# Attention into two MoE layers on one core: later weight decoding, P·V in two pieces per chunk, and the next head pair turned over three units

## The chip, the core and the metric

One core of a Trainium2 chip runs the whole kernel in one launch. The metric is device time in microseconds: the median of three runs before the change is 562.89 us (562.86 to 563.21). Besides these there is one profiled execution, whose instructions, waits and transfers are recorded with their times; it took 561.78 us, of which 559.7 us lie between its first and its last instruction.

## What is computed

```python
def _attn_ref(q, k, v):                       # 2 batches, 8 heads, 576 rows, 64 columns
    ...
    q_rot, k_rot = rotate(q), rotate(k)       # rotary positions
    scores = scale * np.matmul(q_rot, k_rot.transpose(0, 1, 3, 2))
    scores = scores - np.max(scores, axis=-1, keepdims=True)
    attn = np.exp(scores)
    attn = attn / (np.sum(attn, axis=-1, keepdims=True) + 1e-09)
    return np.matmul(attn, v)

def _moe_ref(x, w_in, w_out):                 # 1152 tokens, 512 -> 2048 -> 512
    h = x @ w_in
    g = np.maximum(h, 0.0) + np.log1p(np.exp(-np.abs(h)))
    return g @ w_out
# then _moe2_ref: skip test, gate, 8 experts of 512 -> 1024 -> 512, one expert for each token
```

The weights `w_in` and `w_out` arrive as 64-bit floats, which the kernel takes apart with integer operations ("decoding").

## The kernel before

**Stages.** Attention takes about the first 187 us of the profiled execution, then comes the first MoE layer (class `Moe1`), then the second (class `Moe2`). The change touches attention and the decoding of the first weights.

**Pairs and units.** The 16 heads of both batches are worked on as 8 pairs of heads: pairs 0 to 3 in batch 0, pairs 4 to 7 in batch 1. A pair has five units: four of 128 query rows for both heads (numbers 0 to 3), and one, "m", of the last 64 rows of both heads. There are 40 units, counted 0 to 39. In batch 0 their order is 0, 1, 2, 3, m; in batch 1 it is 2, 3, m, 0, 1. I say first, second, ... unit of a pair for the place in that order.

**One unit.** For each of the two heads a: S, matmuls that write scores into PSUM tile `s` (`s_mm`, L188; two such tiles exist); M, the row maximum on VectorE (`s_max`, L220); E, exp on ScalarE (`s_exp`, L228). One unit later the exponentials P are turned by TensorE in three groups T0 to T2 (`t_steps`, L286, into PSUM tiles `t`, of which there are three) and copied to `pt` by VectorE or ScalarE (H0 to H2, helper L74). The order of these steps inside a loop pass is written out in `ORDER` (L26). TensorE's order in the loop is as written; the other engines' order is set by a list scheduler, and each engine runs its list strictly in order.

**P·V.** Units are gathered in two chunks per pair. When a chunk's P is turned, its product with v is made in five jobs (`pv_mm`, L337; tiles `pv`, `vr`, `vd`), two jobs in each loop pass (the two J in `ORDER`). After the first job row sums are inverted (`norm`, tile `R`), after the fourth they are turned (`norm_out`, tiles `t..n`, `rb`), after the last the result x goes to `xh` and `xl` (`x_out`).

**Turning the next pair.** While a pair is worked on, the next one is prepared (`prepare`, L437): GpSimd rotates q and k (`rope_pair`; tiles `rt`, `rot`), TensorE turns q and k (`tq`, two times four transposes into `tq` tiles) and the last 64 rows (one transpose into a `tr` tile); ScalarE and VectorE split each into a high and a low half (`halves`, L139; tiles `qT`, `kT`, `qm`); then `stacks` (L173) issues eight copies on SyncE's queue from one place of on-chip memory to another, four for tile `qs` (128 KB each) and four for tile `ks` (288 KB each). The S matmuls of the next pair read `qs` and `ks`: the first head's S reads the two copies for a = 0, the second head's S the two for a = 1. `PREP` (L27) says in which unit of the pair each step is written: q and k rotations in the first, all turning and the copies in the second, loads in the fourth.

**First weights.** `Moe1.weights` (L470) loads 128 columns of `w_in` and 128 rows of `w_out` (tile `raw`, two buffers), decodes each on VectorE by L488, L489, L490 into `wt`, and splits it by a cast on ScalarE (L492) and a subtraction on VectorE (L493) into `w`. I call one load of the two a half. `W_AT` (L32) puts the first two weights behind loop passes 27 and 34, but nothing holds the scheduler to it; it places them where it expects their data.

Of the kernel before, what the change touches and what calls it, by code (L numbers as in the profile page):

```python
# [25 lines left out]
ORDER = "S0 R T0 M0 J H0 E0 S1 T1 H1 M1 J T2 H2 E1 Q".split()  # L26
PREP = ("qk", "t", "", "l", "")  # L27
# [3 lines left out]
W_AT = (27, 34)  # L31
# [12 lines left out]
class Attention:  # L44
# [45 lines left out]
    def load_pair(self, b, hp):  # L90
# [8 lines left out]
        self.pr[b, hp] = dict(xn=xn)  # L99
# [51 lines left out]
    def tq(self, b, hp):  # L151
        nc, p = self.nc, self.pr[b, hp]
        ident = self.cst["ident"]
        rot = p["rot"].rearrange("p i j h d -> p i j (h d)")
# [18 lines left out]
    def stacks(self, b, hp):  # L173

        p = self.pr[b, hp]
        qT, kT = p["qT"], p["kT"]
        p["qs"] = qs = self.wq.tile([128, 2, 512], F32R, name=f"qs{b}{hp}", tag="qs", bufs=2)
        p["ks"] = ks = self.wq.tile([128, 2, 2, 576], F32R, name=f"ks{b}{hp}", tag="ks", bufs=2)
        for a in range(2):
            r = slice(64 * a, 64 * a + 64)  # L180
            kc = slice(64 - 64 * a, 640 - 64 * a)
            for o in range(2):
                d = slice(64 * o, 64 * o + 64)
                self.nc.sync.dma_start(qs[d, a, :].bitcast(F32), qT[r, 0 if o == a else 1, :].bitcast(F32))
# [35 lines left out]
    def s_max(self, b, hp, u, a):  # L220
# [7 lines left out]
    def s_exp(self, b, hp, u, a):  # L228
# [12 lines left out]
        if u == "m":  # L241
            nc.gpsimd.tensor_scalar(P[:, 576:640], P[:, 512:576], 1.0, 1.0, op0=ALU.mult, op1=ALU.mult)
# [94 lines left out]
    def pv_mm(self, b, hp, c, z):  # L337
# [4 lines left out]
        if z == 2:  # L342
            nc.tensor.matmul(ps[:, 0:n], lhsT=p["vd"], rhs=pt[:, 4, 0:n], start=False, stop=False, skip_group_check=True)
            return
        i = (0, 1, None, 2, 3)[z]
        with self.tc.manual_schedule(engines={nc.tensor.engine}):
            for a in range(2):
                nc.tensor.matmul(  # L348
                    ps[64 * a : 64 * a + 64, 0:n], lhsT=p["vr"][:, a, i, :], rhs=pt[:, 5 * a + i, 0:n],
                    start=z == 0, stop=z == 4, skip_group_check=True,  # L350
                )
# [24 lines left out]
    def run(self, side=None):  # L376
# [12 lines left out]
        self.tq(0, 0)  # L389
        self.stacks(0, 0)  # L390
# [6 lines left out]
        for i in range(n + 7):  # L397
# [3 lines left out]
            ready, jobs = jobs[:2], jobs[2:]  # L401
# [3 lines left out]
            with order:  # L405
                for step in ORDER:
# [30 lines left out]
    def prepare(self, i, pairs):  # L437
# [3 lines left out]
        if pi + 1 == len(pairs):  # L441
            return
        nxt = pairs[pi + 1]
        for step in PREP[z]:
            if step == "q":
                self.rope_pair(*nxt, 0, g3)
# [730 lines left out]
```

## Time and profile before

| | |
|---|---|
| median of three runs | 562.89 us |
| the profiled execution | 561.78 us |
| its span, first to last instruction | 559.7 us |
| TensorE busy (matmuls) | 508.4 us, 91% |
| VectorE busy | 416.8 us, 74% |
| ScalarE busy | 326.5 us, 58% |
| GpSimd busy | 125.5 us, 22% |
| first S of pair 0, 1, 2, 3 at | 14.84, 34.58, 59.73, 87.68 us |
| first S of pair 4, 5, 6, 7 at | 107.73, 128.45, 148.27, 168.09 us |
| first matmul of the first MoE layer at | 187.02 us |

Shares over the whole span mix stages with different limits. For this change the stretch from 14.84 to 187.02 us counts, and in it the steps from one pair's first S to the next's. The granted clock of TensorE in a stretch is given as a share of 2.4 GHz; 0.50 is the lower of its two levels, 1.2 GHz.

### The profile page before, as it was taken

The numbers are of one execution on the slowest core, as the hardware profiler recorded it, in microseconds if no ns is written. First come the engines' busy times: TensorE is split into PE (matmuls) and PEld (weight loads), VectorE is DVE, ScalarE is ACT, GpSimd is POOL, SyncE is SP. The second block draws the span as 40 slices with busy tenths as digits, with TensorE's granted clock in tenths as the row PEclk, the third lists the DMA queues.
The fourth block names the chain that finished last, engine by engine and source line by source line (L and its number), as shares of the span: only waits on it lengthen the run. The fifth ranks groups of instructions, "written<-read, shape, count | busy, mean of one in ns | idle before, by whom it ended". The sixth has DMA issues, their size and how long they took to land. (4 is left out here: it accounts for less than half of the span.)

```text
span 559.7 us, 8595 instructions
## 1 busy us (share of the span) xinstructions
PE 508.4 (91%) x2858; PEld 394.7 (71%) x2858; DVE 416.8 (74%) x788; ACT 326.5 (58%) x711; POOL 125.5 (22%) x169
## 2 busy tenths in 40 slices
PE   6796969999999978877999999999999899999993
PEld 2664646667667646567889988989897577777772
DVE  7569886766666389998979994474785579887873
ACT  2565545567656265666566674575564378776860
POOL 5766393763411220000000000000020401220111
PEclk9898979999999999999999999999998999999998
DMA  7897473742550024434213430032205615695301
GB/s 184 196 238 191 133 188 104 182 98 66 125 122 2 2 84 150 117 124 138 75 46 116 142 112 0 1 112 77 80 22 193 245 55 187 224 334 180 97 19 36
DMA packets 42500, 67.17 MB, mean 120 GB/s; under 512 B 9312, under 2 KB 23904, under 8 KB 42448
## 3 DMA queue, kind: packets, MB, share of 16 engines
q1 hardware_dynamic: 38672, 59.59, 36.9%
q0 software_dynamic: 1440, 4.20, 2.0%
q10 hardware_dynamic: 2336, 2.74, 1.5%
q8 instruction: 26, 0.43, 0.3%
q14 instruction: 26, 0.21, 0.1%
HBM read 67.30 MB, written 7.15 MB: 133 GB/s over the span
## 5 line engine op out<-in xcount | busy, mean ns | idle before, releaser
L506 PE MATMUL h<-xh,w 128*128 128x320 f32 (+2 forms) x448 | 106.0, 317 | 6.6 <-DVE w L493 2.9
L543 PE MATMUL acc<-w,gh 128*128 128x512 f32 x288 | 76.9, 397 | 9.3 <-ACT gh L533 9.1
L506 PEld LDWEIGHTS h<-xh,w 128*128 128x128 f32 x448 | 75.5, 188 | 13.9 <-DVE w L493 4.8
L764 DVE TENSOR_TENSOR ws<-raw,ws 128x1024 fp32r<-128x1024 f32 x59 | 70.3, 1220 | 16.8 <-ACT ws L762 16.6
L224 DVE TENSOR_REDUCE m<-s 128x1 f32<-128x576 f32 x64 | 47.7, 755 | 27.6 <-PE s L215 23.9
L506 PE MATMUL h<-xl,w 128*128 128x320 f32 (+2 forms) x224 | 68.1, 313 | 0.0
L543 PEld LDWEIGHTS acc<-w,gh 128*128 128x128 f32 x288 | 52.1, 188 | 22.2 <-ACT gh L533 12.4
L237 ACT ACTIVATE P<-s,m 128x576 f32<-128x576 f32 x64 | 47.6, 744 | 29.9 <-DVE m L224 28.3
L302 PE MATMUL t<-ct,P 128*128 128x128 f32 x288 | 49.8, 287 | 15.1 <-DVE qT L146 6.0
L852 PE MATMUL y<-ws,hT 128*128 128x512 f32 x216 | 59.8, 415 | 0.9 <-DVE hT L838 0.2
L762 ACT CAST ws<-raw 128x1024 fp32r<-128x1024 f32 x59 | 59.2, 1060 | 2.3 <-DMA raw<-in_moe_w_dram 2.0
L302 PEld LDWEIGHTS t<-ct,P 128*128 128x128 f32 x288 | 35.1, 145 | 28.4 <-issue 10.6
L852 PEld LDWEIGHTS y<-ws,hT 128*128 128x128 f32 x216 | 39.2, 188 | 13.4 <-DVE ws L764 2.3
L606 POOL TENSOR_SCALAR sc<-lg 128x2 f32<-128x2 f32 (+1 forms) x3 | 0.9, 294 | 212.2 <-DVE lg L589 212.2
L215 PE MATMUL s<-ks,qs 128*128 128x288 f32 x240 | 47.3, 328 | 0.1
L348 PE MATMUL pv<-pt,vr 128*64 128x256 f32 (+1 forms) x256 | 46.0, 443 | 0.8 <-DVE x L358 0.5
L519 ACT ACTIVATE y<-h 128x320 f32<-128x320 f32 (+2 forms) x56 | 25.0, 447 | 36.5 <-PE h L506 32.1
L215 PEld LDWEIGHTS s<-ks,qs 128*128 128x128 f32 x240 | 35.6, 199 | 13.2 <-issue 5.2
L77 ACT COPY pt<-t 128x384 f32<-128x384 f32 x60 | 28.5, 475 | 25.8 <-PE t L302 21.6
L543 PE MATMUL acc<-w,gl 128*128 128x512 f32 x144 | 42.8, 395 | 0.5 <-DVE gl L534 0.4
L506 PEld LDWEIGHTS h<-xl,w 128*128 128x128 f32 x224 | 41.7, 188 | 2.0
L533 ACT CAST gh<-r 128x320 fp32r<-128x320 f32 (+2 forms) x56 | 24.6, 467 | 29.1 <-DVE r L531 29.1
(257 smaller groups left out, 934.8 us busy)
## 6 DMA issues: line engine op xcount, KB each, us to landing
raw<-in_moe_w_dram SPq DMA_DIRECT2D x68, 512.0 KB
ks<-kT SPq DMA_DIRECT2D x32, 288.0 KB
raw<-in_moe_w_in_dram SPq DMA_DIRECT2D x16, 512.0 KB
raw<-in_moe_w_out_dram SPq DMA_DIRECT2D x16, 512.0 KB
qs<-qT SPq DMA_DIRECT2D x32, 128.0 KB
wr<-in_moe_w_dram SPq DMA_DIRECT2D x5, 512.0 KB
x2d<-x SPq DMA_DIRECT2D x9, 256.0 KB
xn<-in_q_dram SPq DMA_DIRECT2D x8, 256.0 KB
```

Source lines behind the costliest of these rows:

```text
L77: self.nc.scalar.copy(out, in_)
L215: nc.tensor.matmul(ps[:, c, 0:288], lhsT=qs[:, a, uc], rhs=ks[:, a, x, 288 * c : 288 * c + 288], start=x == 0, stop=x == 1,)
L224: nc.vector.tensor_reduce(st["m"][:, a : a + 1], st["ps"][a][:, :, 0:288], axis=AX.XY, op=ALU.max, negate=True)
L237: nc.scalar.activation(P[:, 576 * a : 576 * a + 576].rearrange("p (c n) -> p c n", c=2), ps[:, :, 0:288], AF.Exp, bias=m[:, a : a + 1], ac ...
L302: nc.tensor.transpose(ps[:, 128 * i : 128 * i + 128], src, ident)
L348: nc.tensor.matmul(ps[64 * a : 64 * a + 64, 0:n], lhsT=p["vr"][:, a, i, :], rhs=pt[:, 5 * a + i, 0:n], start=z == 0, stop=z == 4, skip_gro ...
L506: nc.tensor.matmul(ps[c][:, 0:m], lhsT=w[:, 0, x, 128 * k : 128 * k + 128], rhs=src[:, k, c0 + m * c : c0 + m * c + m], start=z == 0, stop ...
L519: nc.scalar.activation(y[:, cs[c]], ps[c][:, 0:m], AF.Abs)
L543: nc.tensor.matmul(acc[t], lhsT=g[x][:, 128 * j : 128 * j + 128], rhs=w[:, 1, y, :], start=f == f0 and z == 0, stop=f == f1 and z == 2,)
L762: hi = nc.scalar.copy(w[:, 0], raw)
L764: self.did[T, c] = hi.ins, nc.vector.tensor_sub(w[:, 1], raw, w[:, 0].bitcast(F32)).ins
L852: nc.tensor.matmul(py, lhsT=ht[:, x, o : o + 128], rhs=w[:, y, 512 * j : 512 * j + 512], start=c == 0 and j == 0 and z == 0, stop=c == 3 a ...
```

## The change

1. Decoding of the first two weights is written in four halves behind loop passes 29, 31, 33 and 35, and on VectorE and ScalarE each half is tied to stand behind the last maximum of its pass (`tc.issue_after`).
2. P·V of a chunk is made in two jobs instead of five, one job in each loop pass instead of two: the first is the `vd` product and half of the `vr` products, the second the other half with `norm_out` and `x_out`. The loop has four closing passes instead of seven.
3. The next pair's q, k and last rows are turned in three units. From the third pair of the loop on (pairs 2 to 6 are the current ones): q in the first unit, k in the second, the last rows and the copies of `ks` in the third. While pair 1 is current: second, third, fourth unit. While pair 0 is current: q in the third, k and last rows in the fourth. The copies of `qs` are issued behind q's turn, those of `ks` behind the turn of the last rows.
4. Rotations on GpSimd and loads are made one pair earlier.
5. The copy of 64 columns of P in unit m moves from GpSimd to ScalarE.

```diff
-ORDER = "S0 R T0 M0 J H0 E0 S1 T1 H1 M1 J T2 H2 E1 Q".split()
-PREP = ("qk", "t", "", "l", "")
+ORDER = "S0 R T0 M0 H0 E0 S1 T1 H1 M1 J T2 H2 E1 Q".split()
+PREP = (("xR", "", "q", "krxv", "R"), ("", "q", "k", "rxvR", ""), ("q", "k", "r", "xvR", ""))
...
-W_AT = (27, 34)
+W_AT = (29, 31, 33, 35)
...
+    def tq(self, b, hp, i):
...
+        if i == 0:
+            p["qT"] = t = self.wq.tile([128, 2, 512], F32R, name=f"qT{b}{hp}", tag="qT", bufs=1)
+            p["qs"] = st = self.wq.tile([128, 2, 512], F32R, name=f"qs{b}{hp}", tag="qs", bufs=2)
+            self.halves(t[:, 0], t[:, 1], ps, True)
+            self.stack(lambda a, d: st[d, a, :], lambda a, o, r: t[r, 0 if o == a else 1, :])
+        else:
+            t = self.kt(b, hp)
+            self.halves(t[:, 0, 64:576], t[:, 1, 64:576], ps)
...
+    def stack(self, dst, src):
         for a in range(2):
             r = slice(64 * a, 64 * a + 64)
             for o in range(2):
                 d = slice(64 * o, 64 * o + 64)
+                self.nc.sync.dma_start(dst(a, d).bitcast(F32), src(a, o, r).bitcast(F32))
...
         if u == "m":
-            nc.gpsimd.tensor_scalar(P[:, 576:640], P[:, 512:576], 1.0, 1.0, op0=ALU.mult, op1=ALU.mult)
+            nc.scalar.copy(P[:, 576:640], P[:, 512:576])
...
-        i = (0, 1, None, 2, 3)[z]
+        if z == 0:
+            nc.tensor.matmul(ps[:, 0:n], lhsT=p["vd"], rhs=pt[:, 4, 0:n], start=True, stop=False, skip_group_check=True)
         with self.tc.manual_schedule(engines={nc.tensor.engine}):
+            for i in (2 * z, 2 * z + 1):
+                for a in range(2):
...
-        for i in range(n + 7):
+        for i in range(n + 4):
...
-            ready, jobs = jobs[:2], jobs[2:]
+            ready, jobs = jobs[:1], jobs[1:]
...
-                        jobs += [(b, hp, c, z) for z in range(5)]
+                        jobs += [(b, hp, c, z) for z in range(2)]
...
+        n1, n2, n3 = pair(1), pair(2), pair(3)
+        first = pi == 0 and z < 3
+        for step in PREP[min(pi, 2)][z]:
...
+            if step in "qk" and n1:
+                self.tq(*n1, "qk".index(step))
+            if step == "r" and n1:
+                self.tr(*n1)
+                self.kstack(*n1)
+            if step == "x" and (n2 if first else n3):
+                self.load_pair(*(n2 if first else n3))
...
+            with after():
+                nc.vector.tensor_scalar(tu, hi, 3, 0x3FFFFFFF, op0=ALU.logical_shift_left, op1=ALU.bitwise_and)
...
             def side(i):
                 if i in W_AT:
-                    moe1.weights(W_AT.index(i), wa, st, 2)
+                    k = W_AT.index(i)
+                    moe1.weights(k // 2, wa, st, 2, (k % 2,), lambda: tc.issue_after(att.last.ins))
```

How the lists of instructions move, at the three places that matter. The names are tile and number; `x4` is four matmuls of that form.

TensorE, before, from the turn of pair 2's k and last rows (`tq`, `tr`, in the second unit of pair 1) to pair 2's first S, which reads `ks_596`:

```order
L161 MATMUL tq_580<-ct,rot_509 128x128 x4
L164 MATMUL tr_587<-ct,remr_168 128x128
L302 MATMUL t_613<-ct,P_547 128x128 x3
...
L197 MATMUL s01m_719<-kT_302,qm_112 128x288 x6
L302 MATMUL t_686<-ct,P_621 128x128 x3
L348 MATMUL pv_692<-pt_528,vr_152 64x256 x2
L302 MATMUL t_702<-ct,P_621 128x128 x3
L302 MATMUL t_726<-ct,P_679 128x128 x3
L348 MATMUL pv_692<-pt_528,vr_152 64x256 x2
L215 MATMUL s_755<-ks_596,qs_595 128x288 x4
```

TensorE, with the change, from the turn of the same last rows (now in the fourth unit of pair 1) to pair 2's first two S, which read `ks_639`:

```order
L180 MATMUL tr_690<-ct,remr_168 128x128
L210 MATMUL s01m_724<-kT_405,qm_112 128x288 x6
L315 MATMUL t_731<-ct,P_658 128x128 x3
L315 MATMUL t_741<-ct,P_658 128x128 x3
L360 MATMUL pv_671<-pt_525,vr_152 64x256 x4
L283 MATMUL t01n_753<-ct,R_682 128x128 x2
L315 MATMUL t_762<-ct,P_658 128x128 x3
L228 MATMUL s_770<-ks_639,qs_572 128x288 x4
L315 MATMUL t01m_775<-ct,P01m 128x128 x4
L228 MATMUL s_787<-ks_639,qs_572 128x288 x4
```

Where 17 rows lay between the last rows' turn and the first S, 6 are left. For pair 1 there are 5 and the m scores now stand ahead of the turn; for pairs 3 and 4 there are 11, for pairs 5 and 6 also 11, for pair 7 10.

VectorE, before, in the second unit of pair 1, where the first weights' halves `wt_1835` and `wt_1843` are decoded (lines 488 to 493):

```order
L149 TENSOR_TENSOR kT_572<-tr_587,kT_572 128x2x64
L488 TENSOR_SCALAR wt_1835<-raw_1833 128x512
L489 SCALAR_TENSOR_TENSOR wt_1835<-raw_1833,wt_1835 128x512
L146 SCALAR_TENSOR_TENSOR qm_109<-tr_587,qm_109 64x64
L488 TENSOR_SCALAR wt_1843<-raw_1841 128x512
L224 TENSOR_REDUCE m_617<-s_624 128x1
L490 SCALAR_TENSOR_TENSOR wt_1835<-raw_1833,wt_1835 128x512
L224 TENSOR_REDUCE m_667<-s_657 128x1
L146 SCALAR_TENSOR_TENSOR qm_109<-tr_587,qm_109 64x64
```

VectorE, with the change, behind unit 29, where the same half (`wt_1897`) now stands (lines 514 to 519):

```order
L237 TENSOR_REDUCE m_1855<-s_1860 128x1
L514 TENSOR_SCALAR wt_1897<-raw_1895 128x512
L80 COPY pt_1791<-t_1865 128x3x128
L515 SCALAR_TENSOR_TENSOR wt_1897<-raw_1895,wt_1897 128x512
L80 COPY rb_1881<-t11n_1878 128x256
L271 TENSOR_SCALAR sm_1739<-sm_1739 128x5
L237 TENSOR_REDUCE m_1914<-s_1905 128x1
L516 SCALAR_TENSOR_TENSOR wt_1897<-raw_1895,wt_1897 128x512
L370 TENSOR_TENSOR x_1883<-pv_1813,rb_1881 128x256
L272 RECIPROCAL sm_1739<-sm_1739 128x5
```

All 22 decoding instructions that stood in pairs 1 and 2 (six halves of three, and four subtractions) now stand between the last maximum of unit 29 and the end of unit 39, one to four in a unit, between that unit's own.

## Rows read from the trace of the kernel before

**Rows 1.** Windows from one pair's first S to the next's, pairs 1 to 4, 6, 7.
```profile
core 0: us, PE busy (x) PEld busy (x) DVE busy (x) ACT busy (x) POOL busy (x), PEclk, DMA share, GB/s
34.58:59.73 25.15, 19.95 (x123) 14.09 (x121) 21.31 (x39) 13.69 (x36) 15.65 (x21) 0.86 0.86 223
59.73:87.68 27.95, 22.43 (x132) 15.07 (x130) 24.50 (x48) 13.16 (x35) 18.45 (x20) 0.88 0.58 163
87.68:107.73 20.05, 18.90 (x131) 13.27 (x129) 14.29 (x32) 12.22 (x32) 11.45 (x16) 1.00 0.48 117
107.73:128.45 20.72, 19.51 (x135) 13.81 (x134) 13.29 (x31) 11.36 (x33) 11.41 (x16) 1.00 0.52 125
...
148.27:168.09 19.82, 18.75 (x133) 13.24 (x131) 13.11 (x31) 12.80 (x34) 3.79 (x8) 1.00 0.41 91
168.09:187.02 18.93, 18.93 (x136) 13.49 (x135) 12.32 (x28) 12.56 (x31) 3.79 (x8) 1.00 0.01 2
```

**Rows 2.** Timeline of TensorE: start, us, instruction, idle before and what ended it.
```profile
25.78 0.52 PE L302 MATMUL t<-ct,P 128*128 128x128 f32 x3 [1.76 <-DVE sm L259]
...
28.93 0.55 PE L302 MATMUL t<-ct,P 128*128 128x128 f32 x3 [0.91 <-DVE pt L79]
...
52.10 1.54 PE L302 MATMUL t<-ct,P 128*128 128x128 f32 x6 [4.03 <-DVE qm L146]
...
73.20 0.52 PE L302 MATMUL t<-ct,P 128*128 128x128 f32 x3 [2.64 <-DVE qT L146]
```

**Rows 3.** Groups by line on VectorE, 45.02 to 80 us: busy us, mean ns.
```profile
L489 DVE SCALAR_TENSOR_TENSOR wt<-raw,wt 128x512 uint32<-128x512 uint32 x6 | 6.4, 1075 | 0.1
L490 DVE SCALAR_TENSOR_TENSOR wt<-raw,wt 128x512 uint32<-128x512 uint32 x6 | 5.9, 976 | 0.0
L488 DVE TENSOR_SCALAR wt<-raw 128x512 uint32<-128x512 uint32 x6 | 4.2, 696 | 0.0
L493 DVE TENSOR_TENSOR w<-wt,w 128x512 fp32r<-128x512 f32 x4 | 3.1, 764 | 0.2
```

**Rows 4.** Windows around the half-speed stretches in pairs 1 and 2.
```profile
50.50:57.10 6.60, 5.00 (x19) 3.62 (x20) 5.99 (x12) 3.45 (x9) 3.27 (x6) 0.50 0.76 200
...
74.00:78.00 4.00, 4.00 (x17) 2.66 (x17) 4.00 (x7) 0.68 (x3) 4.00 (x3) 0.57 0.79 162
```

**Rows 5.** Timeline of TensorE, turn of pair 7's last rows, to its first S.
```profile
158.03 0.27 PE L164 MATMUL tr<-ct,remr 128*128 128x128 f32 x1
...
165.02 0.49 PE L302 MATMUL t<-ct,P 128*128 128x128 f32 x3
165.44 1.08 PE L348 MATMUL pv<-pt,vr 128*64 128x256 f32 x8
166.45 0.79 PE L215 MATMUL s<-ks,qs 128*128 128x288 f32 x4
167.08 0.49 PE L302 MATMUL t<-ct,P 128*128 128x128 f32 x3
167.41 0.60 PE L343 MATMUL pv<-pt,vd 128*128 128x256 f32 x2
167.84 0.49 PE L302 MATMUL t<-ct,P 128*128 128x128 f32 x3
168.09 0.78 PE L215 MATMUL s<-ks,qs 128*128 128x288 f32 x4
```

**Rows 6.** Timeline of SyncE's queue, the copies for pair 7.
```profile
157.09 2.66 SPq L184 DMA_DIRECT2D qs<-qT  x4
160.11 3.75 SPq L185 DMA_DIRECT2D ks<-kT  x4
```

**Rows 7.** Window over pair 7's `ks` copies; last two columns DMA share, GB/s.
```profile
161.50:166.80 5.30, 4.73 (x34) 3.14 (x33) 3.18 (x9) 2.56 (x7) 1.74 (x3) 1.00 0.97 213
```

**Rows 8.** Lines 488 and 489 over the whole span: duration ns min/median/max.
```profile
L488 DVE TENSOR_SCALAR wt<-raw x32: 386/426/1346, 45.0 to 312.9; 128x512 uint32<-128x512 uint32 x32
...
L489 DVE SCALAR_TENSOR_TENSOR wt<-raw,wt x32: 678/685/1666, 46.3 to 315.0; 128x512 uint32<-128x512 uint32 x32
```

More of the change, by code (lines that the diff above doesn't have):

```diff
@@ L98, in load_pair @@
             )
-        self.pr[b, hp] = dict(xn=xn)
+        self.pr.setdefault((b, hp), {})["xn"] = xn
     def load_v(self, b, hp):
@@ L341, in pv_mm @@
         ps = self.pv[b, hp, c]
-        if z == 2:
-            nc.tensor.matmul(ps[:, 0:n], lhsT=p["vd"], rhs=pt[:, 4, 0:n], start=False, stop=False, skip_group_check=True)
-            return
-        i = (0, 1, None, 2, 3)[z]
+        if z == 0:
+            nc.tensor.matmul(ps[:, 0:n], lhsT=p["vd"], rhs=pt[:, 4, 0:n], start=True, stop=False, skip_group_check=True)
         with self.tc.manual_schedule(engines={nc.tensor.engine}):
[L347 to L351, printed above, removed]
+            for i in (2 * z, 2 * z + 1):
+                for a in range(2):
+                    nc.tensor.matmul(
+                        ps[64 * a : 64 * a + 64, 0:n], lhsT=p["vr"][:, a, i, :], rhs=pt[:, 5 * a + i, 0:n],
+                        start=False, stop=i == 3, skip_group_check=True,
+                    )
     def x_out(self, b, hp, c):
@@ L388, in run @@
         self.rope_rem(0, (nc.vector,) * 3, 0, 2)
-        self.tq(0, 0)
-        self.stacks(0, 0)
+        for i in range(2):
+            self.tq(0, 0, i)
+        self.tr(0, 0)
+        self.kstack(0, 0)
         if WARM2:
@@ L440, in prepare, with pair @@
         z, pi = i % 5, i // 5
[L441 to L446, printed above, removed]
-                if nxt == (1, 0):
+        def pair(k):
+            return pairs[pi + k] if pi + k < len(pairs) else None
+        n1, n2, n3 = pair(1), pair(2), pair(3)
+        first = pi == 0 and z < 3
+        for step in PREP[min(pi, 2)][z]:
+            if step == "R" and (n1 if first else n2):
+                nx = n1 if first else n2
+                self.rope_pair(*nx, 0, g3)
+                if nx == (1, 0):
                     self.load_rem(1)
-            if step == "k":
-                self.rope_pair(*nxt, 1, g3)
-                if nxt == (1, 0):
+                self.rope_pair(*nx, 1, g3)
+                if nx == (1, 0):
                     self.rope_rem(1, g3)
-            if step == "t":
-                self.tq(*nxt)
-                self.stacks(*nxt)
-            if step == "l" and pi + 2 < len(pairs):
-                self.load_pair(*pairs[pi + 2])
-                self.load_v(*pairs[pi + 2])
+            if step in "qk" and n1:
[5 more added lines that the diff above has]
+                self.load_pair(*(n2 if first else n3))
+            if step == "v" and n2:
+                self.load_v(*n2)
 class Moe1:
@@ L468, in __init__, with weights @@
         self.w = {}
-    def weights(self, f, wp, st, bufs):
+    def weights(self, f, wp, st, bufs, parts=(0, 1), after=nullcontext):
         nc = self.nc
-        w = wp.tile([128, 2, 2, 512], F32R, name=f"w{f}", tag="w", bufs=bufs)
+        if f not in self.w:
+            self.w[f] = wp.tile([128, 2, 2, 512], F32R, name=f"w{f}", tag="w", bufs=bufs)
+        w = self.w[f]
         fs = slice(128 * f, 128 * f + 128)
-        for i in range(2):
+        for i in parts:
             raw = st.tile([128, 512], mybir.dt.int64, name=f"raw{f}{i}", tag="st", bufs=2)
```

56 lines of the change are left out of this document (27 added, 29 removed).

## The prediction

> **What bounds the kernel now.** I began with the windows from one pair's first S to the next's, because shares over the whole span mix attention with two other stages. From pair 3 on, TensorE is busy for nearly the whole step: 18.90 of 20.05 us, 19.51 of 20.72, 18.75 of 19.82 and, in pair 7, all of 18.93, at a granted clock of 1.00 [rows 1]. There TensorE is the bound. Pairs 1 and 2 are different: their steps take 25.15 and 27.95 us, VectorE is busy for 21.31 and 24.50 us of them (13 to 14 in later pairs), and the clock is 0.86 and 0.88 [rows 1]. Next I read TensorE's timeline there: it stands idle for 4.03 us behind VectorE's `qm` and for 2.64 us behind `qT` [rows 2]. The groups on VectorE show why these came late: 22 decoding instructions, 19.6 us in all, lie in this stretch [rows 3]. Last, the windows behind the two idles have a clock of 0.50 and 0.57: TensorE runs at the lower of its levels, 1.2 GHz, after standing idle [rows 4].
>
> **What the change takes away.** (a) Without decoding, pairs 1 and 2 have no reason to differ from pair 3: 25.15 − 20.05 = 5.10 and 27.95 − 20.05 = 7.90, together 13.0 us [rows 1]. (b) TensorE's idles of 1.76 and 0.91 us in pair 0, behind `sm` and `pt` on VectorE [rows 2], go if turning moves out of the way: 2.7 us. (c) Inside the other pairs TensorE idles for 20.05 − 18.90 = 1.15, 1.21 and 1.07 us in pairs 3, 4 and 6 [rows 1]. With q, k and last rows turned in three units rather than at once, its evacuations no longer delay the maxima. At 1.15 for each of pairs 1 to 3, 1.21 for pair 4 and 1.07 for pairs 5 and 6, that is 6.8 us. Sum of credits: 22.5 us. (a) is sure as far as the decoding goes away from there; (b) and (c) are upper bounds, lower bound 0, which the range holds.
>
> **What it costs, first: the copies of `ks`.** They are now issued one or two units later, and the next pair's S stands closer behind. Before, pair 7's last rows are turned at 158.03 us [rows 5], the first `ks` copy is issued at 160.11 and the four issues take 3.75 us [rows 6]: 2.08 us from turn to issue, with q, k and last rows evacuated together. The copies then move at 213 GB/s in 161.5 to 166.8 us [rows 7], which is 1.13 MB, about the four of 288 KB. So two have landed some 4.05 us after the first issue (161.5 + 2.65 − 160.11), all four 6.7 us after. The Trainium skill, "DMA: Bandwidth & Descriptors", section "Where 436 GB/s comes from", gives 435 GB/s for transfers between two places of on-chip memory; by it the four would be there in an estimated 2.7 us in place of 5.3, and the time is rival 4's. The 213 GB/s of rows 7, at a DMA share of 0.97, say otherwise, and I go by them.
>
> With the last rows alone to evacuate I take 1.3 us from turn to issue; the bounds are 0.6 us, less than the 0.94 us between two issues [rows 6], and the 2.08 us of today. Then the first head's S can start 5.35 us after the turn of the last rows, the second head's at 8.0.
>
> What TensorE has to do in between comes from the order lists with the pitches of rows 5: S 0.63 (166.45 to 167.08), a T group about 0.38, eight P·V records of 256 columns 1.01, two vd 0.43, so 0.95 for the six m matmuls (1.5 S), 0.5 for four T, 0.25 for two n. Pair 1: three T groups, P·V, n and the turn 0.13, 2.5 us, so a wait of 2.85 us, then 1.13 us of work (T m, S) and 1.5 us more: 4.35. Pair 2 has the m scores as well, 3.5 us: 1.85 + 1.5 = 3.35. Pairs 3 to 7 have some 6.1 us before the first S, no wait there, and 7.5 us before the second: 0.5 each, 2.5. Together 10.2 us. For pairs 3 to 5, loads of a later pair's rows stand ahead of the copies on SyncE's queue and share its rate; pair 5's also wait for GpSimd's rotation, now one pair earlier. I put them within the 0.5. For pairs 6 and 7 the loads of the second weight wait for the decoding of the first, but stand behind the copies and hold up only decoding.
>
> **Clock.** Waits of 2 to 3 us in pairs 1 and 2 are as long as the 2.64 us after which the clock was 0.57 in a 4.00 us window with TensorE all busy [rows 2, 4]: 4.00 × 0.43 = 1.7 us lost. Twice that: 3.4. Lower bound 0; upper, twice the other stretch (5.00 us busy at 0.50, 2.5 us lost): 5.0. No pair of the trace waits for its `ks`, so the price is taken from these two stretches.
>
> **Short units.** In pairs 4 to 7 the first unit of a pair now holds at times only one P·V job where there were two, and the chain maximum, exp, T of one unit is then less well covered. Bounds: 0, and the idle of a pair today, 1.15 [rows 1]; I take 0.6 in four pairs, 2.4 us.
>
> **Decoding behind units 29 to 35.** All 22 instructions now stand in pairs 6 and 7, where VectorE has 13.11 + 12.32 = 25.4 us of work in 38.75 us [rows 1]. Free of GpSimd (3.79 us busy there, 15.65 and 18.45 in pairs 1 and 2) L488 takes 0.426 and L489 0.685 at the median [rows 8], not 0.696 and 1.075 [rows 3]; with L490 and L493 taken as L489 that makes 6 × (0.426 + 2 × 0.685) + 4 × 0.685 = 13.5 us. VectorE then wants 38.9 of 38.75 us. Lower bound 0: the maxima are first in each pass, P·V and T fill TensorE meanwhile, and a late half is not wanted before 187 us. Upper bound: the whole 13.0 of (a) comes back here. Nearer: with VectorE 85% busy, as in pair 1 (21.31 of 25.15), 38.9 us need 45.8, 7.0 more. In pairs 1 and 2 the turning waited behind a lump, here one to four decoding instructions stand in a unit, so I take half, 3.5.
>
> **Costless.** The copy of P on ScalarE adds an instruction per pair to an engine that is busy for 12 to 13 of 20 us [rows 1]; without that cover it would be a few tenths. The shorter tail gains nothing: the first MoE layer starts with rows of batch 0, long done. GpSimd's earlier rotations lie where it is 15 to 18 of 25 to 28 us busy, without decoding beside them.
>
> **Sum.** Costs 10.2 + 3.4 + 2.4 + 3.5 = 19.5, credits 22.5: −3.0 us against the profiled execution of 561.78 us, so 558.8. The median of the runs, 562.89, lies 1.1 above that execution: forecast **559.9 us**. A measurement of this kernel can tell 0.2%, 1.1 us, from no change.
>
> **Rivals.**
> 1. *The copies are issued as late as now.* If the last rows' evacuation stands behind maxima on VectorE or ScalarE, turn to issue stays 2.08 us and each of seven pairs waits 0.8 us longer (5.5), and the clock costs its upper 5.0 (1.6 more): −3.0 + 7.1 = +4.1, 567.0 us, slower. It decides from about 1.7 us from turn to issue on: 0.43 us more in seven pairs is the 3.0 us of gain. For it: 2.08 us in rows 5 and 6. Against it: that was three evacuations, now one.
> 2. *VectorE is the bound in pairs 6 and 7.* At pair 1's 85%, 7.0 in place of 3.5: +0.5, 563.4 us, no change. With all 13.0 given back: 569.4. For it: 38.9 us of work. Against it: GpSimd is quiet and nothing waits for the decoded weights.
> 3. *The waits are covered and decoding fits.* No clock lost, no decoding cost: −3.0 − 3.4 − 3.5 = −9.9, 553.0 us. For it: pair 7 today has no idle at all at 12.32 us of VectorE [rows 1].
> 4. *The copies move faster when alone.* Traffic starts 1.4 us after the first issue [rows 6, 7]. At twice 213 GB/s two copies land 1.33 us later, all four 2.65: with 1.3 us from turn to issue that is 4.0 and 5.35 us after the turn, so pair 1 waits 1.5 + 0.2, pair 2 0.5 + 0.2, the others not, and no clock is lost: −22.5 + 2.4 + 2.4 + 3.5 = −14.2, 548.7 us. For it: the copies no longer run beside those of q. Against it: a DMA share of 0.97 at 213 GB/s [rows 7]. That is the time by the page named above, were its rate to hold here.
> 5. That the order isn't as described is excluded by the order lists, which show each move.
>
> **How the numbers follow.** Forecast 0.47 (its own range 557 to 563); rival 1 0.10; rival 2 0.14 at 85% and 0.06 in full; rival 3 0.20; rival 4 0.03. Range 552.5 to 566: it leaves out rival 4, the full form of rival 2, the upper half of rival 1 and the edge of rival 3, 0.2. Faster by over 0.2% (under 561.8): 0.37 of the forecast, rivals 3 and 4: 0.60. Within 0.2%: 0.08 of the forecast and 0.08 of rival 2: 0.16. Slower: the rest, 0.24.
>
> **What would show it.** Pair 1's first S at about 36 us, then steps of some 25 and 22.5, later 20; no idle of 4.03 or 2.64 behind `qm` or `qT`; instead idles of 2 to 3 and 1.5 us before the first two S of pairs 1 and 2 that end with a copy, with a half clock behind them; turn to first `ks` issue near 1.3 us; VectorE near full in pairs 6 and 7 with L515 near 0.69 us. Wrong if steps of pairs 3 to 5 grow beyond 21 us, if pairs 6 and 7 grow by more than 5 together, or if pairs 1 and 2 stay above 24.

## The result and the profile after

The change takes 557.82 us (median of four runs, 556.97 to 559.89) against 562.88 us before (four runs): a ratio of 0.9915, 95% interval 0.9888 to 0.9943, so 4.8 us less by the ratio (5.1 by the medians), clear of the 0.2% that can be told. The forecast was 559.9 us, 3.0 less. The profiled execution took 559.89 us with a span of 558.1 us; it is the longest of the four runs, and its late start, told below, is a likely reason.

The windows from one pair's first S to the next's, pairs 0 to 7, after the change; the columns are those of [rows 1]:

```profile
17.86:38.84 20.98, 15.35 (x112) 12.13 (x112) 13.14 (x26) 11.85 (x31) 13.49 (x17) 0.97 0.80 191
38.84:63.84 25.00, 21.46 (x129) 16.44 (x130) 14.54 (x31) 13.09 (x33) 11.83 (x16) 0.82 0.61 167
63.84:85.79 21.95, 20.05 (x126) 15.35 (x127) 13.79 (x28) 12.43 (x32) 12.46 (x17) 0.84 0.46 120
85.79:105.42 19.63, 18.01 (x129) 13.44 (x129) 14.27 (x33) 12.80 (x33) 13.26 (x18) 1.00 0.49 124
105.42:125.23 19.81, 17.62 (x126) 13.11 (x126) 12.92 (x29) 12.67 (x34) 11.18 (x15) 1.00 0.44 102
125.23:144.79 19.56, 17.86 (x131) 13.51 (x130) 13.46 (x31) 12.89 (x34) 8.39 (x11) 1.00 0.44 102
144.79:165.71 20.92, 17.67 (x129) 13.36 (x128) 18.13 (x41) 14.11 (x38) 3.48 (x7) 1.00 0.54 134
165.71:186.87 21.16, 18.10 (x129) 13.51 (x129) 18.11 (x39) 12.80 (x34) 4.58 (x7) 1.00 0.38 117
```

VectorE has 14.54 and 13.79 us of work in pairs 1 and 2, not 21.31 and 24.50, and 18.1 in pairs 6 and 7, not 13.11 and 12.32. Yet pair 1's step is 25.00 us, as long as before (25.15), and its clock is 0.82. TensorE's timeline says what it waits for now; these are its idles of over 0.5 us from 35 to 90 us:

```profile
38.84 1.30 PE L228 MATMUL s<-ks,qs 128*128 128x288 f32 x4 [3.69 <-issue]
41.54 1.30 PE L228 MATMUL s<-ks,qs 128*128 128x288 f32 x4 [0.54 <-issue]
63.84 0.77 PE L228 MATMUL s<-ks,qs 128*128 128x288 f32 x4 [2.99 <-issue]
66.50 1.30 PE L228 MATMUL s<-ks,qs 128*128 128x288 f32 x4 [1.27 <-DMA ks<-kT]
85.79 0.77 PE L228 MATMUL s<-ks,qs 128*128 128x288 f32 x4 [0.62 <-issue]
88.08 0.76 PE L228 MATMUL s<-ks,qs 128*128 128x288 f32 x4 [0.75 <-DMA ks<-kT]
```

Each is one of the first two S of pairs 1, 2 and 3. Where the row names "issue", the profile shows no releaser; but by the trace's records of landings a copy of `ks` landed less than 0.15 us before each of the six, the second copy before the first S of a pair and the fourth before its second S. The turn of the last rows and SyncE's queue before the first two of these pairs:

```profile
32.13 0.27 PE L180 MATMUL tr<-ct,remr 128*128 128x128 f32 x1
...
57.41 0.27 PE L180 MATMUL tr<-ct,remr 128*128 128x128 f32 x1
```

```profile
33.73 3.76 SPq L194 DMA_DIRECT2D ks<-kT  x4
...
58.40 4.20 SPq L194 DMA_DIRECT2D ks<-kT  x4
```

From turn to first issue 1.60 and 0.99 us, from issue to the first S 5.11 and 5.44 us. Three windows, over the first wait and over the two slow stretches:

```profile
35.10:38.84 3.74, 0.05 (x1) 0.03 (x1) 1.45 (x6) 0.70 (x2) 3.74 (x7) 0.81 0.98 210
...
38.84:47.60 8.76, 8.21 (x31) 6.61 (x33) 4.28 (x8) 4.12 (x11) 2.14 (x4) 0.50 0.75 221
66.50:72.00 5.50, 5.50 (x24) 5.24 (x25) 2.47 (x4) 2.94 (x8) 0.00 (x0) 0.54 0.21 48
```

While TensorE waits, the DMA engines are busy for 0.98 of the time and move 210 GB/s; behind the waits TensorE works at a mean clock of 0.50 and 0.54, for 8.21 and 5.50 us.

**Where the time went.** In the profiled executions the steps of the eight pairs together fall by 3.17 us (172.18 to 169.01), and what follows the first matmul of the first MoE layer by about 1.5. But pair 0's first S comes 3.02 us later, 17.86 instead of 14.84. That hides most of the gain in this execution: 559.89 stands only 1.9 us under the 561.78 of before, while from first S to the end it is 544.9 before and 540.2 after, 4.6 or 4.7 less, near what the runs have.

### The profile page after: what moved, and what is told of

Read it like the earlier page. It is cut to its first block, busy times and chain, and to the rows that moved or that the text cites. A ratio compares the mean times of both kernels' runs of the same rounds, so it can differ in the third digit from the quotient of the medians.

```text
span 558.1 us, 8574 instructions
## 1 busy us (share of the span) xinstructions
PE 502.2 (90%) x2858; PEld 397.5 (71%) x2858; DVE 411.2 (74%) x788; ACT 329.3 (59%) x719; POOL 120.3 (22%) x161
## 5 line engine op out<-in xcount | busy, mean ns | idle before, releaser
L568 PE MATMUL acc<-w,gh 128*128 128x512 f32 x288 | 78.3, 403 | 8.9 <-ACT gh L558 8.8
L568 PEld LDWEIGHTS acc<-w,gh 128*128 128x128 f32 x288 | 52.9, 191 | 22.1 <-ACT gh L558 12.1
L228 PE MATMUL s<-ks,qs 128*128 128x288 f32 x240 | 49.3, 334 | 19.2 <-issue 9.3
L315 PE MATMUL t<-ct,P 128*128 128x128 f32 x288 | 46.8, 281 | 0.2 <-DVE kT L150 0.2
L360 PE MATMUL pv<-pt,vr 128*64 128x256 f32 (+1 forms) x256 | 37.9, 418 | 0.0
```

The costliest lines, as they stand in the source:

```text
L228: nc.tensor.matmul(ps[:, c, 0:288], lhsT=qs[:, a, uc], rhs=ks[:, a, x, 288 * c : 288 * c + 288], start=x == 0, stop=x == 1,)
L315: nc.tensor.transpose(ps[:, 128 * i : 128 * i + 128], src, ident)
L360: nc.tensor.matmul(ps[64 * a : 64 * a + 64, 0:n], lhsT=p["vr"][:, a, i, :], rhs=pt[:, 5 * a + i, 0:n], start=False, stop=i == 3, skip_grou ...
L568: nc.tensor.matmul(acc[t], lhsT=g[x][:, 128 * j : 128 * j + 128], rhs=w[:, 1, y, :], start=f == f0 and z == 0, stop=f == f1 and z == 2,)
```

## The experiments

All ratios are to the kernel before, run beside it on the same chip (its medians 563.73, 563.12 and 563.42 us). Intervals are some 0.3% to each side, so that experiments less than some 2.5 us apart aren't told from each other. Where two experiments ran on different chips, the ratios are compared. "Step" is from one pair's first S to the next's.

### The change once more

> The changed kernel as it is, once more. Theory A (chance at the start): in the profiled execution of the change pair 0's first S came at 17.86 us where it came at 14.84 before, because the first loads landed later and the second warming block then ran at half clock; the instructions up to there are the same, so this is a matter of the execution. A second profile then has its first S near 15 us and takes 557 us, with 542 us from first S to the end as in the first one; the median is 557 to 558. Theory B (the earlier loads and rotations of pair 1 hold up the start every time): first S again near 17.9 us, the profile near 560 us.

Measured: 558.51 us, ratio 0.9909 (0.9875 to 0.9943). The first S is at 16.63 us, and 539.4 us lie from there to the end. The expected 15 us did not come, but neither did 17.9. Ten more profiles, below, settle it: with the startup instructions of before, the experiment with late decoding alone has its first S at 18.75 us; over all profiles of this study it lies between 14.84 and 18.75. It is a matter of the execution, and 14.84 of the profile before was the earliest of all. I compare profiles from the first S on.

### Late decoding alone

```diff
 # kernel before
-W_AT = (27, 34)
+W_AT = (29, 31, 33, 35)
...
-                    moe1.weights(W_AT.index(i), wa, st, 2)
+                    k = W_AT.index(i)
+                    moe1.weights(k // 2, wa, st, 2, (k % 2,), lambda: tc.issue_after(att.last.ins))
```

> The kernel before with part 1 of the change alone: the first two weights decoded in four halves behind units 29, 31, 33 and 35. Theory A (decoding is what holds up pairs 1 and 2): their steps fall from 25.15 and 27.95 to about 20 us, 13.0 us less, and pairs 6 and 7 grow by 3 to 4 together: 552 to 555 us, which is faster than the whole change, since no wait for ks comes with it. Theory B (turning q, k and the last rows at once in one unit is what holds them up, decoding only adds to it): steps of 22 to 25 us stay, 557 to 561 us. Theory C (decoding costs late what it cost early): pairs 6 and 7 grow by 8 or more, 562 us or above.

Measured: 549.11 us, ratio 0.9731 (0.9698 to 0.9764), 14.6 us less than before and 9 less than the whole change. The windows of pairs 1, 2, 6 and 7:

```profile
39.20:58.41 19.21, 17.62 (x122) 12.50 (x120) 14.11 (x33) 12.36 (x34) 14.37 (x21) 1.00 0.84 213
58.41:78.47 20.06, 18.93 (x132) 13.28 (x130) 14.30 (x32) 12.24 (x33) 11.75 (x16) 1.00 0.57 135
...
139.07:159.97 20.90, 18.81 (x132) 13.28 (x131) 17.61 (x40) 13.97 (x35) 4.22 (x8) 1.00 0.57 137
159.97:179.88 19.91, 19.18 (x137) 13.52 (x135) 18.85 (x41) 13.39 (x33) 4.57 (x8) 1.00 0.32 99
```

Theory A by the steps: pairs 1 and 2 shed 5.94 and 7.89 us, pairs 6 and 7 grow by 1.08 and 0.98, together less than the 3 to 4 expected. The time is 3 us below the expected 552 to 555. In the profiles 11.1 us of the gain lie in the eight steps and 3.0 behind them, which no experiment ties to a cause. The clock is 1.00 in these four windows (0.82 in pair 0). Turning everything in one unit was no trouble by itself: pair 2 has the step of pair 3.

### Early decoding in the changed kernel

```diff
-W_AT = (29, 31, 33, 35)
+W_AT = (27, 34)
...
-                    moe1.weights(k // 2, wa, st, 2, (k % 2,), lambda: tc.issue_after(att.last.ins))
+                    moe1.weights(W_AT.index(i), wa, st, 2)
```

> The changed kernel with its part 1 undone: first weights written whole behind loop passes 27 and 34 with no tie, so that the scheduler places their decoding in pairs 1 and 2 again. Theory A: pairs 1 and 2 grow, though less than the 13.0 us by which they differed before, since VectorE has slack while TensorE waits for ks: by 5 to 8; pairs 6 and 7 fall from 20.92 and 21.16 to 19.6 each, 2.9 less; 560 to 563 us. Theory B (the waits for ks cover the decoding): pairs 1 and 2 grow by under 2, and the time falls to 555 to 557.

Measured: 561.11 us, ratio 0.9958 (0.9935 to 0.9982).

```profile
38.85:69.17 30.32, 23.73 (x129) 16.55 (x130) 25.10 (x48) 14.80 (x37) 15.36 (x17) 0.83 0.67 188
69.17:93.12 23.95, 21.42 (x127) 16.07 (x127) 16.57 (x34) 12.42 (x32) 12.00 (x14) 0.79 0.64 174
...
152.82:172.44 19.62, 18.00 (x130) 13.54 (x130) 13.20 (x30) 13.00 (x34) 3.48 (x7) 1.00 0.39 88
172.44:191.88 19.44, 17.61 (x127) 13.25 (x127) 11.83 (x27) 11.48 (x30) 3.47 (x7) 1.00 0.08 19
```

Theory A: pairs 1 and 2 grow by 5.32 and 2.00, pairs 6 and 7 shrink by 1.30 and 1.72. So late decoding costs the changed kernel 3.0 us at the end of attention, in the forecast 3.5.

### P·V in five jobs in the changed kernel

```diff
-ORDER = "S0 R T0 M0 H0 E0 S1 T1 H1 M1 J T2 H2 E1 Q".split()
+ORDER = "S0 R T0 M0 J H0 E0 S1 T1 H1 M1 J T2 H2 E1 Q".split()
...
-                        jobs += [(b, hp, c, z) for z in range(2)]
+                        jobs += [(b, hp, c, z) for z in range(5)]
```

(`pv_mm`, the two jobs taken in each pass and seven closing passes as in the kernel before.)

> The changed kernel with its part 2 undone: P V in five jobs, two in each pass, and seven closing passes. Theory A (each change of form on TensorE, from P V over 64 output columns to transposes and scores and back, costs time; two pieces have fewer of them): TensorE's busy time in pairs 3 to 7 returns from 17.6 to 18.1 us to 18.8 to 19.5 us, about 0.9 more for each of eight pairs; where that is the bound the time is 5 to 7 us above the change, 563 to 565. Theory B (TensorE waits for exponentials in those pairs, and more work between two scores only fills the wait): busy time grows as said, idle time shrinks by as much, 557 to 559 us.

Measured: 556.8 us, ratio 0.9884 (0.9841 to 0.9927), not to be told from the change and just under theory B's 557 to 559. Pairs 3, 4 and 5:

```profile
82.36:102.33 19.97, 19.50 (x134) 13.96 (x135) 14.90 (x33) 12.17 (x33) 14.14 (x19) 1.00 0.54 128
102.33:121.87 19.54, 18.77 (x129) 13.18 (x129) 13.64 (x31) 12.24 (x33) 11.23 (x15) 1.00 0.48 107
121.87:141.71 19.84, 18.84 (x133) 13.30 (x131) 13.54 (x31) 13.29 (x35) 8.49 (x11) 1.00 0.45 101
```

Theory B: TensorE is busy for 1.0 to 1.5 us more in each pair than in the windows after the change, and idle for 0.7 to 1.4 less; the steps are the same within 0.4 us. The two pieces do save TensorE work. The P·V groups of pairs 3 to 6, before and after:

```profile
L348 PE MATMUL pv<-pt,vr 128*64 128x320 f32 x64 | 12.1, 458 | 0.3
```

```profile
L360 PE MATMUL pv<-pt,vr 128*64 128x320 f32 x64 | 10.4, 445 | 0.0
```

(Busy time and mean of one record in ns; the fourth number is idle time ahead.) The same 64 records take 1.7 us less. But in the change TensorE then waits, in pair 4 and at the second S of pairs 5, 6 and 7 as follows:

```profile
108.07 0.76 PE L228 MATMUL s<-ks,qs 128*128 128x288 f32 x4 [1.09 <-issue]
110.80 0.80 PE L228 MATMUL s<-ks,qs 128*128 128x288 f32 x4 [0.56 <-ACT P L250]
127.74 0.76 PE L228 MATMUL s<-ks,qs 128*128 128x288 f32 x4 [1.10 <-ACT P L250]
147.50 0.76 PE L228 MATMUL s<-ks,qs 128*128 128x288 f32 x4 [1.29 <-DMA ks<-kT]
168.33 0.76 PE L228 MATMUL s<-ks,qs 128*128 128x288 f32 x4 [0.98 <-ACT P L250]
```

All but the second row are the second S of a pair, and the fourth copy of `ks` landed 0.09 to 0.20 us before each of them (at 107.98, 127.61, 147.37 and 168.13 us); where the row names an exponential, that ended another 0.12 to 0.14 us later. So the time that the two pieces save goes in good part into waits for the copies, and the rest into waits for exponentials. With five jobs, more work stands in front of these S, and no idle at a second S is longer than 0.54 us; but in pairs 5 to 7 that S still starts 0.08 to 0.25 us after the fourth copy has landed, so its time is much the same.

### Late decoding and two jobs

The kernel with late decoding alone, with P·V in two jobs and four closing passes as in the change.

> The kernel before with parts 1 and 2 of the change: late decoding, and P V in two jobs with four closing passes; turning, copies, rotations and loads stay as before. Late decoding alone gave 549.1 us. Theory A (fewer changes of form save TensorE time, but units without P V make it wait for exponentials, and the two cancel): 548 to 551. Theory B (the two jobs save what TensorE's busy time shows, 6 us, because this kernel has no waits for ks): 543 to 545. Theory C (the waits for exponentials cost more than the saving): 552 to 555, and the two jobs are part of why the whole change stays 9 us above its part 1.

Measured: 553.09 us, ratio 0.9819 (0.9779 to 0.9859); theory C by its number. But most of the loss lies in one place, pair 1, whose step is 4.5 us longer than with late decoding alone; pair 4 adds 1.1 (21.82 for 20.71). Pair 1, and TensorE's timeline and GpSimd's there:

```profile
36.59:60.30 23.71, 18.80 (x120) 13.99 (x119) 13.46 (x32) 12.03 (x33) 13.65 (x21) 0.86 0.66 172
```

```profile
38.12 0.76 PE L215 MATMUL s<-ks,qs 128*128 128x288 f32 x4
41.44 0.33 PE L302 MATMUL t00m<-ct,P00m 128*128 128x128 f32 x1 [2.56 <-POOL P00m L242]
41.52 0.77 PE L215 MATMUL s<-ks,qs 128*128 128x288 f32 x4
42.12 0.77 PE L302 MATMUL t<-ct,P 128*128 128x128 f32 x3
44.25 1.33 PE L215 MATMUL s<-ks,qs 128*128 128x288 f32 x4 [1.36 <-ACT P L237]
```

```profile
38.41 0.73 POOL L116 TENSOR_TENSOR rt<-xn,cr 128x256 f32<-128x256 f32 x1 [5.45 <-DMA xn<-in_q_dram]
...
40.45 0.72 POOL L117 TENSOR_TENSOR rt<-xn,cr 128x256 f32<-128x256 f32 x1
41.14 0.24 POOL L242 TENSOR_SCALAR P00m<-P00m 128x64 f32<-128x64 f32 x1
```

The copy of 64 columns of P takes 0.24 us, but stands on GpSimd behind four instructions of a rotation that waited for its load. With late decoding alone the scheduler had put it behind two of the four, and TensorE waited 0.58 us for it. That led to the ninth experiment.

### All turning in the second unit

In the changed kernel:

```diff
-PREP = (("xR", "", "q", "krxv", "R"), ("", "q", "k", "rxvR", ""), ("q", "k", "r", "xvR", ""))
+PREP = (("xR", "qkr", "", "xv", "R"), ("", "qkr", "", "xvR", ""), ("", "qkr", "", "xvR", ""))
```

> The changed kernel with its part 3 undone: q, k and last rows are all turned in the second unit of a pair, with the copies of qs and ks behind them, rotations and loads stay one pair earlier. Theory A (part 3 is what costs: waits for ks of 2 to 4 us before pairs 1 and 2, and TensorE at 1.2 GHz behind them): no wait for ks is left, the steps of pairs 1 and 2 fall from 25.0 and 22.0 to 20 us, 548 to 551 us. Theory B (the earlier rotations and loads, or the copy of P on ScalarE, cost it): 555 to 559. Theory C (turning at once stalls TensorE now that P V is in two pieces): waits for ks go, idles behind qT and qm of 1 to 2 us in each pair come, 553 to 556.

Measured: 547.93 us, ratio 0.9734 (0.9696 to 0.9773).

```profile
39.56:58.44 18.88, 16.35 (x121) 12.68 (x119) 13.29 (x32) 12.46 (x35) 10.67 (x15) 1.00 0.71 184
58.44:78.40 19.96, 17.54 (x132) 13.45 (x131) 14.19 (x30) 12.66 (x33) 11.29 (x15) 1.00 0.57 132
```

Theory A: no wait for `ks` is left, and the steps of pairs 1 and 2 are 18.88 and 19.96 us, with a clock of 1.00 in both, 8.1 us less than in the change together. Part 3 is what holds the change up. It isn't all loss, though: pairs 0 and 4 take 22.21 and 21.87 us here, 1.2 and 2.1 more than in the change, and TensorE stands idle for 0.99 us behind `qT` in pairs 1 to 3 again.

### Turning in the first and second unit

In the changed kernel:

```diff
-PREP = (("xR", "", "q", "krxv", "R"), ("", "q", "k", "rxvR", ""), ("q", "k", "r", "xvR", ""))
+PREP = (("xR", "q", "kr", "xv", "R"), ("q", "kr", "", "xvR", ""), ("q", "kr", "", "xvR", ""))
```

> The changed kernel with the turning one to two units earlier: q in a pair's first unit (for pair 1: the second), k, last rows and the copies of ks in its second (for pair 1: the third). Theory A (waits for ks cost, split turning is worth something): copies land before the next pair in all pairs but at most pair 1, and 546 to 550 us, below the change with all turning in the second unit. Theory B (split turning is worth nothing): the same as that one within 1.5 us. Theory C (in the first unit q's turn waits for VectorE behind the last pair's work and TensorE with it): 552 or more.

Measured: 546.64 us, ratio 0.9722 (0.9688 to 0.9756). Pairs 2 to 6 have steps of 19.14 to 19.53 us, shorter than with all turning in the second unit, but the median lies within the interval of that one: A and B are not told apart, C falls.

### Late decoding and later copies

In the kernel with late decoding alone, the four issues of `ks` are written in the fourth unit of pairs 0 and 1 and in the third of the others.

> The kernel before with part 1 (549.1 us) and one more thing: the four ks copies are issued later, in the fourth unit of pairs 0 and 1 and in the third of the others, as in the change; everything is turned in the second unit as before. Theory A (the place of the ks copies is what costs): waits for ks of 1.5 to 4 us before pairs 1 and 2, half clock behind them, 554 to 558 us. Theory B (the place of the copies costs little, since without the turn of the last rows ahead of them they are issued at once): 549 to 551 us.

Measured: 551.11 us, ratio 0.9792 (0.9762 to 0.9822), a tenth above theory B's range. It tests less than I meant: SyncE's queue had nothing to wait for ahead of these issues and made them at 32.30 and 53.07 us for pairs 1 and 2, some 3 to 4.5 us behind the turn of the last rows, not a unit or two later. The place of an issue in the list is not its time. In the change the issues follow the turn of the last rows by 0.99 to 1.63 us, so what makes the copies late there is the turn.

### Late decoding, two jobs, and the copy of P on ScalarE

In the kernel with late decoding and two jobs:

```diff
-            nc.gpsimd.tensor_scalar(P[:, 576:640], P[:, 512:576], 1.0, 1.0, op0=ALU.mult, op1=ALU.mult)
+            nc.scalar.copy(P[:, 576:640], P[:, 512:576])
```

> The kernel before with parts 1, 2 and 5 of the change: late decoding, two jobs, and the copy of 64 columns of P on ScalarE; turning, rotations and loads as before. With parts 1 and 2 alone (553.1 us) pair 1's T m waited 2.56 us for that copy on GpSimd, which stood behind a rotation, and a wait of 1.36 us and half clock followed. Theory A (that copy is the price): pair 1's step falls from 23.7 to 20 us, 548 to 550 us. Theory B (the wait only shows what is late anyway; the earlier rotations of part 4 are what helps): 552 to 554.

Measured: 547.04 us, ratio 0.9704 (0.9667 to 0.9741).

```profile
38.83:57.70 18.87, 16.36 (x120) 12.70 (x119) 13.28 (x32) 12.43 (x35) 13.38 (x19) 1.00 0.85 205
```

Theory A, 1 us below its range: pair 1's step is 18.87 us at a clock of 1.00. One copy of 0.24 us on the wrong engine cost 4.8 us in that step, 6 in the medians, through TensorE's wait and the clock behind it. This kernel differs from the one with all turning in the second unit by part 4 and the order in which copies are issued; their ratios, 0.9704 and 0.9734, are not told apart, so no gain or loss from the earlier rotations and loads shows.

### Only pairs 1 and 2 turned earlier

In the changed kernel:

```diff
-PREP = (("xR", "", "q", "krxv", "R"), ("", "q", "k", "rxvR", ""), ("q", "k", "r", "xvR", ""))
+PREP = (("xR", "q", "kr", "xv", "R"), ("q", "kr", "", "xvR", ""), ("q", "k", "r", "xvR", ""))
```

> The changed kernel, with the turning of pairs 1 and 2 alone made earlier (q in the second and first unit, k, last rows and copies of ks in the third and second); pairs 3 to 7 are turned in three units as in the change. Earlier turning in all pairs gave 546.6 us against 558.5. Theory A (the price is the waits for ks of 3.7 and 3.0 us before pairs 1 and 2 and TensorE at 1.2 GHz behind them): 9 of those 12 us are gained, 549 to 551 us. Theory B (small waits in each of the later pairs add up to as much): 552 to 555.

Measured: 545.42 us, ratio 0.9694 (0.965 to 0.9737), some 12 us under the change. Pairs 0 to 2:

```profile
18.05:34.93 16.88, 14.96 (x109) 11.73 (x108) 11.65 (x23) 11.28 (x30) 13.27 (x16) 1.00 0.91 221
34.93:55.09 20.16, 18.11 (x128) 13.34 (x128) 14.39 (x31) 12.42 (x32) 11.79 (x16) 1.00 0.79 191
55.09:74.27 19.18, 18.09 (x133) 13.74 (x132) 14.39 (x32) 13.07 (x36) 12.60 (x16) 1.00 0.60 163
```

Theory A, and more than it expected: all of the 12 us are gained, not 9. The first S of pair 1 waits 0.18 us instead of 3.69, the second 1.22, the clock stays at 1.00, and these three steps take 56.2 us where the change took 67.9: 11.7 us, of which TensorE's idle time is 6.0 and its busy time 5.7. Pairs 3 to 7, turned as in the change, stay where they were, within 0.4 us each.

### Earlier turning, and decoding spread over three pairs

```diff
-W_AT = (29, 31, 33, 35)
+W_AT = (24, 27, 30, 33)
```

(In the kernel with turning in the first and second unit.)

> The changed kernel with earlier turning in all pairs (546.6 us) and the four halves decoded behind units 24, 27, 30 and 33 instead of 29, 31, 33 and 35. Theory A (VectorE, busy for 17.6 to 18.1 us in pairs 6 and 7 and 13.5 in pair 5, makes exponentials late at the end; spread over three pairs the same work costs nothing): 542 to 545 us. Theory B (what VectorE has to do there is covered): 546 to 547.5. Theory C (decoding that starts earlier frees the load buffers earlier, and the third weight's decoding moves into the place that was cleared): 546 to 548 and VectorE as busy in pairs 6 and 7 as before.

Measured: 544.36 us, ratio 0.9655 (0.9622 to 0.9689), the fastest of the study and 14 us under the change. By the profile it is no clear case for A: pairs 5, 6 and 7 take 21.08, 19.27 and 21.76 us, 62.1 together, against 60.6 with decoding behind 29 to 35 (19.26, 19.15, 22.14), VectorE is busy for 18.05, 16.73 and 15.26 us, and in pair 7 the clock is 0.92, as it was with that one. The 2.3 us between the two medians are hardly more than the runs' spread. What lowers the clock in pair 7 of both was not tried. The step of 21.39 us in pair 7 of the kernel with late decoding, two jobs and the copy on ScalarE has a clock of 0.92 too, while that of the kernel with all turning in the second unit has 1.00 and 19.84 us behind the same two idles of 0.95 and 0.62 us; so these idles alone do not decide it.

## Why the prediction was right, and where it was not

Its sign and its range were right, and so was the main mechanism: decoding leaves pairs 1 and 2, and waits for `ks` with a half clock behind them come in its place. That the sum (−3.0 us, measured −4.8) came so near is in part luck, because errors of both signs met: the copies and the clock cost some 8 us more than forecast, and a saving of TensorE's work that was not in the sum stood against it. By steps, from the terms of the sum: forecast and measured changes of the eight pair steps against the windows of before.

| step of pair | forecast, us | measured, us |
|---|---|---|
| 0 | −2.7 + 2.85 = +0.15 | +1.24 |
| 1 | −5.10 − 1.15 + 1.5 + 1.7 + 1.85 = −1.20 | −0.15 |
| 2 | −7.90 − 1.15 + 1.5 + 1.7 = −5.85 | −6.00 |
| 3 | −1.15 + 0.5 = −0.65 | −0.42 |
| 4, 5 | −2.28 + 1.0 + 1.2 = −0.08 | −0.91 and −0.26 |
| 6, 7 | −1.07 + 1.0 + 1.2 + 3.5 = +4.63 | +1.10 and +2.23 |
| sum | −3.0 | −3.17 |

The prediction's list of signs does not quite follow from its own terms: it named 25 and 22.5 us for the steps of pairs 1 and 2, and about 36 us for pair 1's first S, where the terms give 23.95, 22.1 and 34.7. It also called itself wrong if pairs 1 and 2 stayed above 24 us: pair 1 did, at 25.00, not because decoding still held it up but because of the waits and the clock, which were larger than forecast.

- **(a), the 13.0 us of decoding in pairs 1 and 2: right, and shown.** Alone it takes 5.94 + 7.89 = 13.8 us off these two steps. `qm`'s 4.03 us and `qT`'s 2.64 us [rows 2] are gone.
- **(b), the 2.7 us of idles in pair 0: right.** The idles behind `sm` and `pt` are gone after the change; one of 0.45 us for an exponential has come.
- **Decoding behind units 29 to 35, 3.5 us: right.** 3.0 us by the experiment that undoes it, 2.1 by the one that makes it alone. L515 takes 0.682 us there in the mean. Rival 2 (VectorE as the bound) is out: at 18.1 of 21 us it is as busy as in pair 1 of before (85%), without the stall that went with it there.
- **The copies of `ks`: right in kind, too low in size.** From turn to issue it is 0.99 us for pair 2 and 1.48 to 1.63 for the others, forecast 1.3. The time from the first issue to the landings was misread: 4.05 us for two copies and 6.7 for four assumed that the window of [rows 7] holds all the traffic and that two copies have landed when half of it has moved. By the records of landings it was 5.05 and 7.60 us for the same copies before the change, and it is 5.0 to 5.4 and 7.6 to 8.0 in the seven pairs after it. So pairs 1 and 2 waited 4.23 and 4.26 us at their first two S (forecast 4.35 and 3.35), and pairs 3 to 7 1.37, 1.37, 1.10, 1.29 and 1.32 (forecast 0.5 each): 14.9 us of idle time, not 10.2. Pair 1 came near by chance: its first wait was longer than forecast, its second shorter, since the S and T ahead of that one ran at half clock. Rival 1, whose turn to issue was 2.08 us, did not come, though 1.63 lies near the 1.7 from which it would have decided. Rival 3 is out, since the waits came. Rival 4 is out: 210 GB/s at a DMA share of 0.98, with TensorE idle. The Trainium skill gives 435 GB/s as the bound for such transfers in "DMA: Bandwidth & Descriptors", "Where 436 GB/s comes from"; these copies moved at 210 and 213 GB/s in the two windows shown. Why they stay at half of it, no run here shows.
- **The clock: mis-sized.** Forecast were twice 1.7 us, at most 5.0. The slow stretches hold 8.21 us of work at 0.50 and 5.50 at 0.54, which is 4.1 and 2.5 us lost, 6.6 together, above the upper bound. I took the price of a stretch as long as those of [rows 4]; the stretch behind 3.69 and 0.54 us of idle was longer. Waits and clock of pairs 1 and 2 come to 15.1 us, against 11.1 in the forecast (7.7 of waits, 3.4 of clock). Turning these two pairs earlier gives back 11.7 of them in three steps, since other idles, such as the 1.22 us at pair 1's second S, stand there then.
- **(c), the 6.8 us of idles inside the pairs: wrong.** They didn't go. In pairs 3 and 4 TensorE idles for 1.62 and 2.19 us where it idled for 1.15 and 1.21. The idles behind `qT` and `qm` went, but others stand in their place: in pair 3 0.75 us for `ks` and 0.57 for an exponential, in pair 4 1.09 for `ks`, 0.56 for an exponential and 0.53 for a copy to `pt` on ScalarE. The 2.4 us of "short units" can't be told apart from these.
- **Two pieces of P·V: a credit I had not seen, and that was not paid out.** I costed them at nothing but short units. They take 0.9 and 1.9 us of TensorE's busy time off pairs 3 and 4, and the five-job experiment shows that the steps do not get shorter by it: the waits for `ks` and for exponentials take it back. This nearly cancels the idles of (c), which is why the later pairs came out close. Where the copies land in time, with turning in the first and second unit, the steps of pairs 2 to 6 are 19.1 to 19.5 us against 19.8 to 20.9 with late decoding alone; what of this is the two jobs and what the split turning was not tried apart.
- **The copy of P: costed at nothing, wrongly.** In the kernel with late decoding and two jobs it was worth 5 to 6 us. I asked what it costs on ScalarE and not what it was waiting behind on GpSimd. What it is worth in the whole change, where rotations come earlier, was not tried.
- **Start and end.** The first S at 17.86 us is a matter of the execution. The 1.5 us less behind 186.87 us were not forecast and stay open: over the profiles of this study that part takes 367.1 to 372.9 us in no order that I could tie to a part of the change (372.9 with five jobs, 367.1 with early decoding).

So most of the gain of the change, 14.6 us by its first part alone, was given back by its third: copies one or two units later, which cost most before the two pairs that had the least work in front of their first S.

## What to carry to other kernels

When work is taken off the engine that was late, moving what waited for it is a second change with its own price: make the first alone, and see whether the second is still wanted. Splitting a step over more units spreads its load but moves its end, and a transfer behind that end wants its own time (here some 6.5 us from the last turn to the first use) in front of the first reader, in the shortest pair and not in the average one. A tiny copy on an engine whose list is held up by loads can cost far more than its own time (here 5 to 6 us for 0.24).

## What was not expected of the hardware

- Time at the lower clock behind a wait was not of one length: 8.21 us of work behind idles of 3.69 and 0.54 us, 5.50 (at 0.54) behind 2.99 and 1.27. After the 2.99 us idle before pair 2 the next S still ran in 0.77 us, its full speed; only after the next idle, 1.27 us, did it take 1.30.
- P·V records of one form cost less in longer rows: 64 of them took 12.1 us of the profile's busy time in groups of four, 10.4 in groups of eight.
- The landings of the four `ks` copies kept their distance: the second came 5.0 to 5.4 us after the first issue, the fourth 7.6 to 8.0, for pairs 5 to 7 before the change and for all seven pairs after it.
- The start took between 14.84 and 18.75 us to the first S in thirteen profiles. In the one of the change TensorE waited 2.91 us (1.89 before) for a rotation whose load came late, and the twelve warming matmuls behind it took 4.44 us (2.75).
